# Column groups instead of token tiles: the order of the products that pick up the leader's rows of the last batch

## The chip, the cores and the metric

The kernel runs on one core of a Trainium2 chip. The metric is the device time of one execution in microseconds (us), as the median of several executions. The profile is of one execution of its own. The engines have one instruction stream each: TensorE (PE in the rows; its weight loads are the rows PEld), VectorE (DVE), ScalarE (ACT), GpSimd (POOL) and SyncE (SP, which here issues DMAs only). A letter q behind an engine's name is its sequencer, which issues DMAs.

## The reference

Three stages follow each other, all in float32.

```python
# 1. attention, batch 4, heads 8, sequence 576, head size 64
scores = scale * q @ k.T + min(-(cum[:, None] - cum[None, :]), 0)   # causal; cum = cumsum(max(s, 0))
attn   = softmax(scores);  x = (attn @ v)                           # -> [2304 tokens, 512]
# 2. eight experts, each token goes to one of them
e = argmax(x @ w_gate);  p = softmax(x @ w_gate)[e]
x = p * (max(x @ w1[e], 0) @ w2[e])                                 # w1 512x1024, w2 1024x512
# 3. dense
h = max(x @ w_in, 0);  out = (h * h) @ w_out                        # 512 -> 2048 -> 512
```

## The kernel before

**Three stages in one program.** The attention stage (class `Attention`) works through four batches of 576 tokens. The expert stage (class `Moe`, `run`) takes the experts one after the other, with a fixed room of columns for each (400 for the first, then 360, 336 and so on), in eight steps of 128 hidden units: `l1` (lines L1460 to L1462) makes twelve products `he`, `act1` (L1469, L1470) turns them into the operands `hhe` and `hle`, `l2` (L1479 to L1481) makes twelve products `y_e`. The dense stage has the same form (`hd`, `y_d`). In these stages the order of the instructions on each engine is the order in which the code is written.

**Float32 in two parts.** Every float32 operand of a product is split into a high part, which ScalarE copies, and a low part, which VectorE makes by subtracting the high part from the source. A product then needs high with high, high with low, and low with high. `split` (L1389 for the high part, L1390 for the low) does it for the weights of the next step: `wae_1h`, `wae_1l` are the parts of the first expert's second block of w1, `wbe_1h`, `wbe_1l` of w2.

**The first expert starts early.** The expert with the most tokens in the first three batches, the leader, goes first, so that its tokens of those batches can be fetched before the gate of the last batch is done. That is what `Moe.first` does. The leader's 400 columns of x, transposed, are built in four banks of PSUM, `acc(k)` for k from 0 to 3, one for each 128 of the 512 features; in the rows they are `ttacc` (k = 0, 1) and `pvacc` (k = 2, 3). First a product with zeros opens each bank (L1266). Then the rows fetched from the first three batches are turned into place by products with a diagonal of ones (`s4aux`, tasks `xgt`). Last come the rows of the fourth batch, still in SBUF: the tasks `take` multiply their features by a matrix `Pones` of zeros and ones, 256 columns wide, that VectorE makes from the tokens' places (task `at`, L1323). There are five tiles t of tokens, four of 128 (features `xhb`, `xlb`) and one of 64 (`hhb`, `hlb`), hence ten products for each k, all on line L1262. Then ScalarE makes the high part `xhf` of each bank (tasks `xh`, L1341) and VectorE the low part `xlf` (tasks `xl`, L1344): these are the x that the first products `he` read.

The features' own parts are made before: ScalarE makes `xhb`, `hhb` by column group c (tasks `bh`, L1310), VectorE the low parts `xlb`, `hlb` (tasks `bl`, L1313, two for each c). VectorE makes the last batch's places with the chain of the gate: `g_lg`, `g_oh`, products `ork` on TensorE, `base`, `g_slot`, `slots`. It also makes the order of the other seven experts (tasks `order`, L1056 to L1090, and `order2`, L1097 to L1104), which SyncE reads before it fetches the next expert's token list (`idt`).

**What sets the order there.** The tasks of the attention stage and of `Moe.first` are put in order by a planner (`Steps.run`), at build time. Each task has an engine, an estimated duration, the tasks that it needs, the buffers that it uses and a due time; a task inherits an earlier due time from those that need it. The planner keeps a clock of its own, takes the engine with the earliest free task, and of those that can start within 60 ns of each other the one due first. Where TensorE would wait for more than 250 ns of the planner's time, it puts in products that nobody reads (the filler, L330: `ofill`, 256 columns, from `mrow` and `identb`, written off at 110 ns each), as many as fill 80% of the gap.

**Waits in the program.** An engine works its stream in order. A task's needs set the planner's order only; the waits in the program follow from what an instruction reads and writes.

Of the kernel before, what the change touches and what calls it, by code (L numbers as in the profile page):

```python
# [30 lines left out]
class Steps:  # L31
# [37 lines left out]
    def run(self):  # L69
# [37 lines left out]
        while ready:  # L107
# [8 lines left out]
            for e, l in best.items():  # L116
# [4 lines left out]
                            key=lambda x: x[1]["due"])  # L121
                first.append((t, op["due"], e, op))
            t, _, e, op = min(first, key=lambda x: x[:2])
            gap = t - free[e] if e == "PE" and self.fill and not any(self.keep) else 0
            if gap > self.GAP:
# [878 lines left out]
class Moe:  # L1004
# [192 lines left out]
    def first(self, at):  # L1197
# [4 lines left out]
        b, C, N = at.B - 1, CAPS[0], self.NTOK  # L1202

        LO = C - 256
        assert LO * E <= b * at.S
        V = nc.vector
        due = at.PACE * (at.NH + self.LATE)
# [48 lines left out]
        ua = lambda k: ("pv" if k // 2 else "tt", ("acc", k))  # L1256
        left = [2 * (len(self.chunks(C)) + 5)] * 4

        def put_in(k, cols, w, ones):

            left[k] -= 1
            nc.tensor.matmul(out=at.tile(*ua(k))[:, cols], lhsT=w[:, 128 * k:128 * k + 128], rhs=ones,  # L1262
                             start=False, stop=not left[k])

        for k in range(4):
# [6 lines left out]
               need=["leadr"] + put(b - 1), use=[("idt", 0)])  # L1272
# [3 lines left out]
        for c, m in self.chunks(C):  # L1276
            st.add(("xg", c), {"Pool": 1040}, lambda c=c, m=m: self.gather("f", got["idt"], c, m, b * at.S, xg()[:, c]),
                   need=["idt"] + [("gx", i, j) for i in range(b) for j in range(2)], use=[("idt", 0), ug], lat=3000)
            w = "ab"[c // 2]
            h, l = (lambda w=w, x=x, c=c: at.tile(w + x, ("x", c), [128, 512], F32R) for x in "hl")  # L1280
            u = [(w + x, ("x", c)) for x in "hl"]
            at.act(("xgh", c), 540, lambda c=c, m=m, h=h: nc.scalar.copy(out=h()[0:m], in_=xg()[0:m, c]),
                   need=[("xg", c)], use=[ug, u[0]])
            at.dve(("xgl", c), 560, lambda c=c, m=m, h=h, l=l: V.tensor_tensor(
                out=l()[0:m], in0=xg()[0:m, c], in1=h()[0:m].bitcast(F32), op=ALU.subtract), need=[("xgh", c)],
                use=[ug] + u, due=due)
# [15 lines left out]
        for c in range(4):  # L1302
# [13 lines left out]
            ub = [("xb", b), ("xh", "b"), ("hh", "b")]  # L1316
# [3 lines left out]
        ones = lambda t: at.tile("P", ("ones", t), [128, 512], F32R)[:, LO:C]  # L1320
        up = lambda t: ("P", ("ones", t))
        for t in range(5):
            at.dve(("at", t), 140, lambda t=t: V.tensor_scalar(  # L1323
                out=ones(t), in0=places(), scalar1=at.slot[:, t:t + 1], scalar2=None, op0=ALU.is_equal),
                need=["places", ("g", "slot", b)], use=[up(t), ug])

        def take(t, k):
            for x in "hl":
                w = at.tile("x" + x, "b")[:, t, :] if t < 4 else at.tile("h" + x, "b")[0:64]
                put_in(k, slice(LO, C), w, ones(t)[0:w.shape[0]])  # L1330

        ub = [(x + y, "b") for x in "xh" for y in "hl"]
        bl = [("bl", c, i) for c in range(4) for i in range(2)]
        for t in range(3):
            at.pe(("take", t), 8 * 256, lambda t=t: [take(t, k) for k in range(4)], need=[("at", t)] + bl + [("zero", k) for k in range(4)],
                  use=ub + [up(t)] + [ua(k) for k in range(4)])
        x = lambda: got.setdefault("x", None) or got.update(x=self.xtiles("f")) or got["x"]
        for k in range(4):
            at.pe(("take", 3, k), 4 * 256, lambda k=k: [take(t, k) for t in (3, 4)],
                  need=[("at", t) for t in (3, 4)] + bl + [("take", 0)], use=ub + [up(3), up(4), ua(k)])  # L1340
            at.act(("xh", k), C, lambda k=k: nc.scalar.copy(out=x()[0][:, k, 0:C], in_=acc(k)),  # L1341
                   need=[("take", 3, k)] + [("take", t) for t in range(3)] + [("xgt", c, k) for c, _ in self.chunks(C)],
                   use=[ua(k), ("xh", 0)])
            at.dve(("xl", k), C, lambda k=k: V.tensor_tensor(out=x()[1][:, k, 0:C], in0=acc(k),  # L1344
                                                             in1=x()[0][:, k, 0:C].bitcast(F32), op=ALU.subtract),
                   need=[("xh", k)], use=[ua(k), ("xh", 0), ("xl", 0)], due=due)

        for g in range(2):
            for i in range(2):
                at.dma(("w", g, i), lambda eng, g=g, i=i: self.wload(0, g, got["e"], parts=(i,), eng=eng), 1460, queues=("ACT",),  # L1350
                       need=["leada"] + after, use=[("s4", (g, i))], due=due + 20000 * g)
        self.ws = {}
        for i, w in enumerate("ab"):
            use = [("s4", (0, i))]
            t = lambda h, w=w: at.tile(w + h, "w", [128, 512], F32R)
# [3 lines left out]
            def low(i=i, t=t, vw=vw, src=src):  # L1359
# [4 lines left out]
                   need=[("w", 0, i)], use=use + [(w + "h", "w")])  # L1364
# [34 lines left out]
    def dense_load(self, i):  # L1399

        nc = self.nc
        NP = self.F2 // 128
        first, f = i < NP, i % NP
        src, dst = (self.w_in, self.win) if first else (self.w_out, self.wout)
        if first:
            dst = dst[:, :, 128 * f:128 * f + 128]
            view = src[:, 128 * f:128 * f + 128].rearrange("(k p) f -> p k f", p=128)
        else:
            dst = dst[:, f, :].unsqueeze(1)
            view = src[128 * f:128 * f + 128, :].unsqueeze(1)  # L1410
        if src.dtype not in (mybir.dt.int64, mybir.dt.uint64):
            nc.sync.dma_start(out=dst, in_=view)
            return
        n = dst.shape[1]

        if i < 2 * NP - 4:
            at = 2 * (i % (NP // 2)) if first else NP - 4 + 2 * (i % 2)
            st = self.wout[:, at:at + 2, :].rearrange("p a d -> p (a d)").bitcast(I32)
        else:
            st = self.s4.tile([128, 1024], I32, tag="s4", name=f"f64_{i}")  # L1420
        st = st.rearrange("p (n m t) -> p n m t", n=n, t=2)
        nc.sync.dma_start(out=st.rearrange("p n m t -> p n (m t)"), in_=view.bitcast(I32))
        self.f64[i] = (st, dst)
# [50 lines left out]
    def l2(self, key, hh, hl, C, acc, first, last):  # L1474
        nc = self.nc
        _, (wh, wl) = self.wq.pop(key)
        for m in range(4):
            c = slice(128 * m, 128 * m + 128)
            nc.tensor.matmul(out=acc[m][:, 0:C], lhsT=wh[:, c], rhs=hh[:, 0:C], start=first, stop=False)  # L1479
            nc.tensor.matmul(out=acc[m][:, 0:C], lhsT=wh[:, c], rhs=hl[:, 0:C], start=False, stop=False)  # L1480
            nc.tensor.matmul(out=acc[m][:, 0:C], lhsT=wl[:, c], rhs=hh[:, 0:C], start=False, stop=last)  # L1481
# [264 lines left out]
```

## Time and profile before

| | us |
|---|---|
| median of 3 executions | 914.91 |
| lowest, highest | 914.04, 917.18 |
| the profiled execution, whole time | 913.02 |
| its span, first to last instruction | 911.4 |
| TensorE busy | 841.1 (92%) |
| VectorE busy | 662.0 (73%) |
| ScalarE busy | 494.8 (54%) |
| GpSimd busy | 325.8 (36%) |
| granted TensorE clock, mean | 0.970 of full speed |

The profiled execution lies 1.9 us below the median and its span 1.6 us below its own time, so differences are read from the trace and applied to the median. A line such as `245.60 0.41 PE L1262 MATMUL ttacc<-Pones,xhb 128*128 128x256 f32 x1` is one instruction, or a run of equal ones: start, duration from the first start to the last end, engine, line of the program, operation, what is written and read, shape, count; in square brackets the idle time of the engine just before it and what ended that. Since products are pipelined, the distance between two starts tells what one costs, not the duration printed. The place of the change lies between 239 and 255 us of the span.

### The profile page before, as it was taken

The numbers are of one execution on the slowest core, as the hardware profiler recorded it, in microseconds if no ns is written. First come the engines' busy times: TensorE is split into PE (matmuls) and PEld (weight loads), VectorE is DVE, ScalarE is ACT, GpSimd is POOL, SyncE is SP. The second block draws the span as 40 slices with busy tenths as digits, with TensorE's granted clock in tenths as the row PEclk, the third lists the DMA queues.
The fourth block names the chain that finished last, engine by engine and source line by source line (L and its number), as shares of the span: only waits on it lengthen the run. The fifth ranks groups of instructions, "written<-read, shape, count | busy, mean of one in ns | idle before, by whom it ended". The sixth has DMA issues, their size and how long they took to land. (4 is left out here: it accounts for less than half of the span.)

```text
span 911.4 us, 17086 instructions
## 1 busy us (share of the span) xinstructions
PE 841.1 (92%) x6451; PEld 714.9 (78%) x6451; DVE 662.0 (73%) x1214; ACT 494.8 (54%) x1001; POOL 325.8 (36%) x354
## 2 busy tenths in 40 slices
PE   4888868877999999999999999999999999999994
PEld 3566656656799999999999778888888888888894
DVE  8989988996859789888988884544464456444673
ACT  4779758886444444554555444544454444444562
POOL 9876667575355436554522540100010002000100
PEclk9999988988899999999999999999999999999998
DMA  6787978940576586677562300000000001000100
GB/s 146 146 153 172 165 142 174 190 98 18 167 235 192 160 265 195 211 234 265 188 200 73 116 1 1 15 33 1 1 34 13 1 1 47 1 1 1 47 1 26
DMA packets 155489, 94.03 MB, mean 103 GB/s; under 512 B 115292, under 2 KB 140342, under 8 KB 155402
## 3 DMA queue, kind: packets, MB, share of 16 engines
q1 hardware_dynamic: 143410, 78.00, 32.8%
q0 software_dynamic: 4096, 10.19, 3.4%
q10 hardware_dynamic: 7896, 4.69, 1.8%
q8 instruction: 52, 0.85, 0.4%
q14 instruction: 35, 0.29, 0.1%
HBM read 70.16 MB, written 10.02 MB: 88 GB/s over the span
## 5 line engine op out<-in xcount | busy, mean ns | idle before, releaser
L1599 POOL DMA_INDIRECT out_dram<-o,ids x18 | 18.5, 1025 | 342.0 <-ACT o L1596 299.1
L1542 DVE TENSOR_TENSOR sqd<-hd,rld 128x512 f32<-128x512 f32 (+1 forms) x80 | 50.9, 636 | 112.9 <-ACT rld L1540 112.1
L1540 ACT ACTIVATE rld<-hd 128x512 f32<-128x512 f32 (+1 forms) x80 | 44.4, 555 | 129.6 <-PE hd L1462 126.8
L1546 DVE TENSOR_TENSOR ald<-sqd,ahd 128x512 fp32r<-128x512 f32 (+1 forms) x80 | 51.1, 639 | 51.5 <-ACT ahd L1545 50.8
L1545 ACT CAST ahd<-sqd 128x512 fp32r<-128x512 f32 (+1 forms) x80 | 46.3, 579 | 75.4 <-DVE sqd L1542 75.4
L722 POOL TENSOR_TENSOR L<-P,H 128x512 f16<-128x512 f32 x59 | 72.4, 1239 | 27.2 <-ACT H L721 22.0
L1442 POOL TENSOR_TENSOR lf<-lf,pw 128x512 f32<-128x512 f32 x32 | 50.1, 1567 | 73.9 <-DVE pw L1441 55.3
L719 ACT ACTIVATE P<-tt 128x512 f32<-128x512 f32 x96 | 54.5, 595 | 19.7 <-PE tt L667 17.5
L755 PE MATMUL pv<-v,H 128*128 128x65 f16 (+1 forms) x896 | 59.0, 199 | 4.4 <-ACT xb L785 1.8
L1469 ACT ACTIVATE hhe<-he 128x400 fp32r<-128x400 f32 (+7 forms) x64 | 27.9, 436 | 61.7 <-PE he L1462 61.5
L755 PEld LDWEIGHTS <-H 128*128 128x128 f16 x896 | 50.0, 100 | 11.2 <-issue 8.0
L755 PE MATMUL pv<-v,L 128*128 128x65 f16 x448 | 55.2, 197 | 3.4 <-issue 1.4
L667 PE MATMUL tt<-qB,kB 128*128 128x128 f16 (+3 forms) x352 | 57.5, 238 | 0.0
L721 ACT CAST H<-P 128x512 f16<-128x512 f32 x96 | 56.6, 619 | 1.2 <-DVE v L449 0.8
L666 PE MATMUL tt<-qA,kA 128*128 128x128 f16 (+3 forms) x352 | 53.7, 239 | 1.6 <-ACT P L719 1.4
L755 PEld LDWEIGHTS <-L 128*128 128x128 f16 x448 | 43.9, 103 | 4.1 <-issue 1.5
L601 DVE TENSOR_REDUCE tops<-mxb 128x1 f32<-128x128 f32 (+1 forms) x96 | 43.5, 499 | 4.8 <-remote 2.6
L1167 POOL DMA_INDIRECT xg<-x_dram,idt x20 | 20.8, 1040 | 69.5 <-PE xps L1177 63.7
L577 PE MATMUL mxb<-kB,qB 128*128 128x128 f16 (+3 forms) x128 | 33.6, 325 | 12.2 <-ACT qB L499 4.8
L1470 DVE SCALAR_TENSOR_TENSOR hle<-he,hhe 128x400 fp32r<-128x400 f32 (+7 forms) x64 | 30.8, 480 | 13.8 <-ACT hhe L1469 12.9
L667 PEld LDWEIGHTS <-kB 128*128 128x128 f16 x368 | 34.0, 105 | 8.4 <-issue 4.1
L666 PEld LDWEIGHTS <-kA 128*128 128x128 f16 x368 | 35.0, 105 | 6.4 <-issue 2.5
(699 smaller groups left out, 3072.6 us busy)
## 6 DMA issues: line engine op xcount, KB each, us to landing
w0s<-in_moe_w_dram SPq DMA_DIRECT2D x30, 512.0 KB
w1s<-in_moe_w_dram SPq DMA_DIRECT2D x30, 512.0 KB
wout<-in_moe_w_in_dram SPq DMA_DIRECT2D x16, 512.0 KB
wout<-in_moe_w_out_dram SPq DMA_DIRECT2D x12, 512.0 KB
ldq<-in_q_dram SPq DMA_DIRECT2D x31, 128.0 KB
ldv<-in_v_dram SPq DMA_DIRECT2D x28, 128.0 KB
ldk<-in_k_dram SPq DMA_DIRECT2D x27, 128.0 KB
x_dram<-xb SPq DMA_DIRECT2D x3, 1024.0 KB
```

The lines of the kernel that those rows point to most:

```text
L601: nc.vector.tensor_reduce(out=st[:, at:at + k], in_=ps[:, c:c + w].rearrange("p (k w) -> p k w", k=k), axis=AX.X, op=ALU.max)
L666: nc.tensor.matmul(out=ps, lhsT=kA[:, j], rhs=qA[:, i], start=not on, stop=False)
L667: nc.tensor.matmul(out=ps, lhsT=kB[:, j], rhs=qB[:, i], start=False, stop=not (mask or more))
L719: self.act(("P",) + key, w, lambda: nc.scalar.activation(out=P(), in_=ps(), func=AF.Exp, scale=0.125), need=[T], use=[use, ("P", key), ("H ...
L721: self.st.add(("H",) + key, {"ACT": 0.833 * w + 80}, lambda: nc.scalar.copy(out=H(), in_=P()), need=[("P",) + key], use=[("P", key), ("H", ...
L722: f = lambda e="Pool": (nc.gpsimd if e == "Pool" else nc.vector).tensor_tensor(out=L(), in0=P(), in1=H(), op=ALU.subtract)
L755: nc.tensor.matmul(out=ps[0:M, I, 0:N], lhsT=a, rhs=m, start=(i == 0), stop=(i == len(ops) - 1))
L1442: nc.gpsimd.tensor_tensor(out=lf, in0=lf, in1=pw.bitcast(F32), op=ALU.mult)
L1540: nc.scalar.activation(out=rl[:, 0:n], in_=ps, func=AF.Relu)
L1542: nc.vector.tensor_tensor(out=a[:, 0:n], in0=ps, in1=rl[:, 0:n], op=ALU.mult)
L1545: nc.scalar.copy(out=ah[:, 0:n], in_=a[:, 0:n])
L1546: nc.vector.tensor_tensor(out=al[:, 0:n], in0=a[:, 0:n], in1=ah[:, 0:n].bitcast(F32), op=ALU.subtract)
```

## The change

The products that pick up the last batch's rows are grouped by column group k instead of by token tile t. Before, three tasks did t = 0, 1, 2 for all four k, eight products each, and four tasks did t = 3 and 4 for one k each; all of them needed the low parts of all four column groups. Now there are four tasks of ten products, one for each k, with t from 0 to 4 inside; each needs all five matrices of ones, but the low parts of its own column group only. The due times of the four low parts `xl` are set apart by 4,000 ns and earlier than before. Number, shape and operands of the products are the same.

```diff
-        def take(t, k):
-            for x in "hl":
-                w = at.tile("x" + x, "b")[:, t, :] if t < 4 else at.tile("h" + x, "b")[0:64]
-                put_in(k, slice(LO, C), w, ones(t)[0:w.shape[0]])
+        def take(k):
+            for t in range(5):
+                for x in "hl":
+                    w = at.tile("x" + x, "b")[:, t, :] if t < 4 else at.tile("h" + x, "b")[0:64]
+                    put_in(k, slice(LO, C), w, ones(t)[0:w.shape[0]])
 
         ub = [(x + y, "b") for x in "xh" for y in "hl"]
-        bl = [("bl", c, i) for c in range(4) for i in range(2)]
-        for t in range(3):
-            at.pe(("take", t), 8 * 256, lambda t=t: [take(t, k) for k in range(4)], need=[("at", t)] + bl + [("zero", k) for k in range(4)],
-                  use=ub + [up(t)] + [ua(k) for k in range(4)])
         x = lambda: got.setdefault("x", None) or got.update(x=self.xtiles("f")) or got["x"]
         for k in range(4):
-            at.pe(("take", 3, k), 4 * 256, lambda k=k: [take(t, k) for t in (3, 4)],
-                  need=[("at", t) for t in (3, 4)] + bl + [("take", 0)], use=ub + [up(3), up(4), ua(k)])
+            at.pe(("take", k), 10 * 256, lambda k=k: take(k), need=[("at", t) for t in range(5)] + [
+                ("bl", k, i) for i in range(2)] + [("zero", k)], use=ub + [up(t) for t in range(5)] + [ua(k)])
             at.act(("xh", k), C, lambda k=k: nc.scalar.copy(out=x()[0][:, k, 0:C], in_=acc(k)),
-                   need=[("take", 3, k)] + [("take", t) for t in range(3)] + [("xgt", c, k) for c, _ in self.chunks(C)],
+                   need=[("take", k)] + [("xgt", c, k) for c, _ in self.chunks(C)],
                    use=[ua(k), ("xh", 0)])
             at.dve(("xl", k), C, lambda k=k: V.tensor_tensor(out=x()[1][:, k, 0:C], in0=acc(k),
                                                              in1=x()[0][:, k, 0:C].bitcast(F32), op=ALU.subtract),
-                   need=[("xh", k)], use=[ua(k), ("xh", 0), ("xl", 0)], due=due)
+                   need=[("xh", k)], use=[ua(k), ("xh", 0), ("xl", 0)], due=due - 4000 * (4 - k))
```

The planner answers to this on three engines; SyncE and GpSimd keep their order, and behind the first products `he` every engine has the order of before.

On TensorE, behind the products `ork` of the gate, stand fillers and then the products of the takes. Before there are 22 fillers, and the first takes go through the four banks:

```order
L330 LDWEIGHTS identb_120
L330 MATMUL ofill_1657_5304<-mrow_129,identb_120 128x256
L1262 MATMUL ttacc_0_5096<-Pones_0_5296,xhb_5031 128x256
L1262 MATMUL ttacc_0_5096<-Pones_0_5296,xlb_5118 128x256
L1262 MATMUL ttacc_1_5099<-Pones_0_5296,xhb_5031 128x256
L1262 MATMUL ttacc_1_5099<-Pones_0_5296,xlb_5118 128x256
L1262 MATMUL pvacc_2_5102<-Pones_0_5296,xhb_5031 128x256
```

Now there are 12 fillers, and the takes go through the five tiles for the first bank:

```order
L1262 MATMUL ttacc_0_5087<-Pones_1_5289,xhb_5022 128x256
L1262 MATMUL ttacc_0_5087<-Pones_1_5289,xlb_5109 128x256
L1262 MATMUL ttacc_0_5087<-Pones_2_5291,xhb_5022 128x256
L1262 MATMUL ttacc_0_5087<-Pones_2_5291,xlb_5109 128x256
L1262 MATMUL ttacc_0_5087<-Pones_3_5293,xhb_5022 128x256
L1262 MATMUL ttacc_0_5087<-Pones_3_5293,xlb_5109 128x256
L1262 MATMUL ttacc_0_5087<-Pones_4_5297,hhb_5023 128x256
L1262 MATMUL ttacc_0_5087<-Pones_4_5297,hlb_5110 128x256
L1262 MATMUL ttacc_1_5090<-Pones_0_5285,xhb_5022 128x256
```

Ten fillers went, and the 64-row products, which stood in the last 16 of the 40, now end each group of ten.

On VectorE, from the end of the gate's chain to the first product's low weights, stand before (the low parts of the features, the matrices of ones, the low weights of the first step, `order` and `order2`, the low parts of x):

```order
L1313 TENSOR_TENSOR xlb<-xb_4237,xhb 128x4x128 x2
L1313 TENSOR_TENSOR hlb<-xb_4237,hhb 64x128 x4
L1323 TENSOR_SCALAR Pones_5296<-xbg,g_slot_5160 128x256
L1360 TENSOR_TENSOR alw<-w0s_0_5208,ahw 128x512
L1360 TENSOR_TENSOR blw<-w1s_0_5218,bhw 128x512
L1056 TENSOR_TENSOR key_5368<-base,base_63 128x8
L1097 CAST nf<-o_n 128x8
L1104 CAST o_off<-off 128x8
L1344 TENSOR_TENSOR xlf<-ttacc_5096,xhf 128x400
L1344 TENSOR_TENSOR xlf<-pvacc_5125,xhf 128x400
L1390 TENSOR_TENSOR wae_1l<-w0s_0_5208,wae_1h 128x512
```

and now:

```order
L1323 TENSOR_SCALAR Pones_5285<-xbg,g_slot_5151 128x256
L1313 TENSOR_TENSOR hlb<-xb_4237,hhb 64x128
L1357 TENSOR_TENSOR alw<-w0s_0_5208,ahw 128x512
L1341 TENSOR_TENSOR xlf<-ttacc_5087,xhf 128x400
L1341 TENSOR_TENSOR xlf<-ttacc_5090,xhf 128x400
L1357 TENSOR_TENSOR blw<-w1s_0_5218,bhw 128x512
L1341 TENSOR_TENSOR xlf<-pvacc_5093,xhf 128x400
L1056 TENSOR_TENSOR key_5382<-base,base_63 128x8
L1341 TENSOR_TENSOR xlf<-pvacc_5116,xhf 128x400
L1097 CAST nf<-o_n 128x8
L1104 CAST o_off<-off 128x8
L1387 TENSOR_TENSOR wae_1l<-w0s_0_5208,wae_1h 128x512
```

The matrices of ones moved ahead of the low parts of the second to the fourth column group (the first group's `hlb` even ahead of the products `ork`); three low parts of x moved ahead of `order`, the fourth ahead of `order2`, so that `order2` now stands directly before `wae_1l`. Lines behind the edited place are three lower now.

On ScalarE one thing moved: the load of the leader's number into a register (L1233, from `lead`), before between the copies `xT` and the first `xhb`, now ahead of the last copy `bhx`, and still ahead of the first loads of w1 and w2:

```order
L1282 CAST bhx_5137<-xbg 128x512
L1233 TENSOR_LOAD lead
L1233 ISA x2
L1282 CAST bhx_5204<-xbg 16x512
L1377 ISA
L1377 DMA w0s_0_5208<-in_moe_w_dram 128x4x256
```

## Rows read from the trace of the kernel before

**Rows 1.** Busy time by stretch, behind the place: us; PE, PEld, DVE, ACT, POOL; clock; DMA.

```profile
252.00:300.00 48.00, 48.00 (x275) 47.86 (x275) 35.95 (x56) 22.98 (x43) 24.29 (x16) 1.00 0.71 220
400.00:500.00 100.00, 97.04 (x723) 93.45 (x723) 87.00 (x138) 54.15 (x108) 40.98 (x31) 1.00 0.57 182
```

**Rows 2.** Timeline of TensorE at the place.

```profile
241.08 4.81 PE L330 MATMUL ofill<-mrow,identb 128*128 128x256 bf16 x22 [0.49 <-DVE base L932]
245.60 0.41 PE L1262 MATMUL ttacc<-Pones,xhb 128*128 128x256 f32 x1
245.85 0.28 PE L1262 MATMUL ttacc<-Pones,xlb 128*128 128x256 f32 x1
245.97 0.28 PE L1262 MATMUL ttacc<-Pones,xhb 128*128 128x256 f32 x1
...
249.36 0.38 PE L1262 MATMUL ttacc<-Pones,xhb 128*128 128x256 f32 x1
...
250.22 0.39 PE L1262 MATMUL pvacc<-Pones,xhb 128*128 128x256 f32 x1
...
251.73 0.27 PE L1262 MATMUL pvacc<-Pones,hlb 64*128 64x256 f32 x1
251.93 0.45 PE L1460 MATMUL he<-xhf,ahw 128*128 128x400 f32 x1
...
254.60 0.34 PE L1462 MATMUL he<-xhf,wae_1l 128*128 128x400 f32 x1
```

**Rows 3.** Busy time and granted clock by stretch, at the place.

```profile
238.00:239.00 1.00, 1.00 (x10) 0.93 (x9) 0.88 (x7) 0.24 (x1) 0.00 (x0) 0.94 0.55 201
240.00:241.00 1.00, 0.58 (x20) 0.50 (x19) 0.50 (x4) 0.99 (x2) 0.00 (x0) 0.50 0.63 217
245.00:246.00 1.00, 1.00 (x8) 0.81 (x7) 1.00 (x3) 0.00 (x0) 1.00 (x1) 0.65 1.10 400
250.00:251.00 1.00, 1.00 (x6) 0.68 (x5) 0.72 (x2) 0.49 (x1) 0.00 (x0) 1.00 0.02 1
```

**Rows 4.** Timeline of VectorE at the place.

```profile
240.62 0.20 DVE L931 TENSOR_TENSOR g_s<-ork,base 128x40 f32<-128x40 f32 x1 [0.47 <-PE ork L928]
...
241.47 1.28 DVE L1313 TENSOR_TENSOR xlb<-xb,xhb 128x512 fp32r<-128x512 f32 x2
242.67 0.88 DVE L1313 TENSOR_TENSOR hlb<-xb,hhb 64x128 fp32r<-64x128 f32 x4
243.48 1.53 DVE L1323 TENSOR_SCALAR Pones<-xbg,g_slot 128x256 fp32r<-128x256 f32 x5
244.94 0.68 DVE L1360 TENSOR_TENSOR alw<-w0s,ahw 128x512 fp32r<-128x512 f32 x1
...
246.15 0.15 DVE L1056 TENSOR_TENSOR key<-base,base 128x8 f32<-128x8 f32 x1
...
247.42 0.17 DVE L1097 CAST nf<-o_n 128x8 f32<-128x8 int32 x1
...
248.50 0.17 DVE L1104 CAST o_off<-off 128x8 int32<-128x8 f32 x1
249.99 0.57 DVE L1344 TENSOR_TENSOR xlf<-ttacc,xhf 128x400 fp32r<-128x400 f32 x1 [1.32 <-issue]
...
253.08 0.69 DVE L1390 TENSOR_TENSOR wae_1l<-w0s,wae_1h 128x512 fp32r<-128x512 f32 x1
```

**Rows 5.** Timeline of ScalarE (and its DMA issues, ACTq) at the place.

```profile
234.26 0.40 ACTq L1380 DMA_DIRECT2D w0s<-in_moe_w_dram  x1
...
235.39 1.13 ACT L1282 CAST bhx<-xbg 128x512 fp32r<-128x512 f32 x2
...
249.47 0.49 ACT L1341 CAST xhf<-ttacc 128x400 fp32r<-128x400 f32 x1 [8.32 <-PE ttacc L1262]
...
261.43 0.61 ACT L1389 CAST wae_4h<-w0s 128x512 fp32r<-128x512 f32 x1
```

**Rows 6.** Timeline of SyncE's DMA issues at the place.

```profile
250.74 0.38 SPq L1160 DMA_DIRECT2D idt<-tab  x1
```

## The prediction, made before the changed kernel ran

> **What bounds the kernel now.** I read the stretches first. Behind 252 us TensorE is busy for 48.00 of 48 us and later for 97 of 100, at full clock, in an order that the change leaves alone [rows 1]. So the change is worth what it moves the first product of that stage, the first `he` at 251.93 [rows 2], less what TensorE then waits for in its first few steps. Next I read TensorE's timeline just ahead of it. 22 fillers run from 241.08 to 245.60 at (245.60 − 241.08)/22 = 0.205 us each; the 40 takes follow from 245.60 to 251.93, 6.33 us, and ScalarE, idle for 8.32 us, starts the first high part of x at 249.47 [rows 2, 5]. Third, what the takes waited for: VectorE has the last low part done at 242.67 + 0.88 = 243.55 and the first matrix of ones by about 243.8 [rows 4]. Nothing held the takes between 243.8 and 245.60 but the fillers ahead of them on TensorE's own stream. The reader is to see there that a wait was covered by more work than the wait was long. Why: the granted clock is 0.50 there, the lower level of 1.2 GHz. It is 0.94 on the mean of 238 to 239, 0.50 from then on, and 0.65 on the mean of 245 to 246, so it fell at about 238.9 and rose at 245.7 (0.3 of that us at full clock) [rows 3]. Ahead of the rise TensorE issued 256-column products without a gap for 4.6 us. The planner wrote the fillers off at 110 ns, and they took 205.
>
> **The change, part by part.** All sums are in the profiled execution, 913.02 us with a span of 911.4; they are carried over to the median of 914.91 as differences.
>
> *Start of the takes.* The products `ork` and the chain on VectorE ahead of the fillers are the same; the one thing put in, the first group's `hlb` (0.2 us each, 0.88 for four), fits into the 0.47 us for which VectorE waits for `ork` [rows 4]. If it did not fit, the fillers would start up to 0.2 us later. So 12 fillers run from 241.08 to 241.08 + 12 × 0.205 = 243.55. Is the data there? Places are done when VectorE goes on at 241.47; five matrices of ones take 1.46 us (243.48 to 244.94), so the last stands at 243.0 and each is ready before TensorE asks for it. Takes start at 243.55 instead of 245.60, 2.05 us earlier; the fillers still hold them.
>
> *The takes themselves.* At full clock they cost 6.20 us: 6.08 from 245.85 to 251.93 and 0.12 for the first, as the pair from 245.85 to 245.97 shows; the 0.25 us of the first itself is still at the lower clock [rows 2]. A change between 128-row and 64-row products costs extra: one round of two and two takes 0.86 us (249.36 to 250.22) against 4 × 0.12 = 0.48. There are four such rounds in both orders, so the 6.20 us stay, 1.55 for each k. Now the first 2.15 us, up to the rise at 245.7, pass at half clock and do 1.07 us of that work. 5.13 us remain: the takes end, and `he` may start, at 250.83, 1.10 us earlier than 251.93.
>
> *The clock's rise* is the unknown in this. I take 245.7 as before, because TensorE issues 256-column products without a gap from 241.08 on in both kernels; only what they multiply changes at 243.55. The bounds are a rise at the start of the takes, which saves another 1.07 us, and none until the takes are through, which is the slow rival below. In the Trainium skill, "TensorE: Matmul & The Clock Gate", Part 1, the clock is throttled by default and released by busy time, not by a number of matmuls, and the moment varies from run to run. By that rule ten fillers fewer do not put off the rise, and the sum stays at 250.83, while other executions would spread around it; the trace, with one rise in this place, agrees with the first part and cannot show the second.
>
> *High and low parts of x.* Each bank is now complete by itself, 1.55 us apart instead of 0.86. By the sums the takes for k = 3 start at 249.28 and their last product ends at 250.9; ScalarE's copy (0.49 us, idle before) is done at 251.43. VectorE has by then the low parts for k = 0 to 2 behind it, the third at 249.4 + 0.04 + 0.49 + 0.04 + 0.57 = 250.5. Then stands `order`, seven small operations, 246.15 to 247.42, of which some 1.15 us hold up what comes next [rows 4]; the fourth low part runs from 251.6 to 252.15. The first `he` needs it only for its eleventh product, at 250.83 + 10 × 0.19 = 252.7 (0.19 us apiece, from (254.60 − 251.93)/14 in [rows 2]). So this is hidden, with 0.5 us to spare.
>
> *What is late next: `wae_1l`.* Behind the fourth low part stands `order2`, from 247.42 to 248.50 + 0.08, 1.16 us [rows 4]. Before it ran in VectorE's idle time ahead of 249.99. Now it ends at 253.25, and `wae_1l` follows at 253.25 to 253.94, later than before (253.08) although the takes end earlier. TensorE asks for it in its fifteenth product, 2.67 us behind the first `he` (251.93 to 254.60): at 253.50. It waits 0.45 us, until 253.95, against 254.60 before. Gain: **0.65 us**. Behind that VectorE has free time (35.95 of 48 us busy) and the steps go on as before [rows 1].
>
> *ScalarE's register load* moves behind the copies `bhx`. In the old place nothing shows of it, and here ScalarE's sequencer runs ahead: it issued the load of `w0s` at 234.26 while the copies before it in the stream still ran from 235.39 to 236.5, 2.2 us later [rows 5]. I take nothing. The bounds are nothing and some 0.5 us on the chain to the places, which would shift the fillers' start by as much; a gain is not in it, as VectorE has work all the time there.
>
> *SyncE.* The token list of the next expert was fetched at 250.74 [rows 6]; its register load reads `order`, which is now done at about 251.6 instead of 247.4. So that fetch and the load of `w0s` queued behind it come 1 to 2 us later. That block is first used at 261.43 [rows 5]: hidden by some 7 us. GpSimd loses nothing: its next work waits for the takes' buffers, which come free earlier.
>
> Sum: 913.02 − 0.65 = 912.4 in the profiled execution, 914.91 − 0.65 = **914.3** as median. That is 0.07%. A measurement of this kernel tells about 0.3% (2.7 us) from no change, and the three executions alone are 3.1 us apart.
>
> **The rivals.**
> *The whole 1.1 us arrives*: `order2` delays nothing, because VectorE catches up while TensorE works through `he`. For it: the small operations can overlap; against: seven of them in a row depend on each other, with 0.2 us between starts. Time 914.91 − 1.10 = 913.8.
> *The wait only changes its name*: `wae_1l` comes at or behind 254.6 because `order` and `order2` both stand between the low parts of x and it, and the chain of copies slips by 0.65 us. For it: VectorE has no idle time left between 250 and 254 by my sum; against: it has to slip further than any row shows. Time 914.9.
> *The clock stays down* (the slower side): the 64-row rounds, now spread through the takes, count for less than fillers, and the rise comes only when the takes are through. Then 2 × 6.20 = 12.4 us put the first `he` at 243.55 + 12.4 = 255.95, 4.0 us later: 918.9. It decides from a rise at 247.9: there (247.9 − 243.55)/2 of the work is lost to the lower clock and `he` starts at 251.93 as before. For it: ten products of certain effect at the place of the rise are gone. Against: from 249.36 to 251.73 the same rounds ran, and the clock stayed at 1.00 [rows 3].
> By the same rule of the Trainium skill ("TensorE: Matmul & The Clock Gate", Part 1) this rival does not come, since 64-row products keep the engine busy too; no row shows a rise during such products.
>
> **How the numbers follow.** Forecast (gain of 0.3 to 0.9 us) 0.45; the whole gain or a little more 0.20; the wait changes its name (gain of −0.3 to 0.3) 0.25; the clock stays down for all or part of the takes 0.10. All but the far end of the last lie within 0.3%. Faster by over 0.3% would need 2.7 us, which no term reaches: only the scatter of executions can give it, 0.05. Slower by over 0.3% has the far end of the last case and the scatter, 0.05. Within 0.3%: 0.90. For the range I take the terms' own (−1.1 to +0.3 us, some way towards +4.0) and the scatter of the three executions (0.9 below and 2.3 above the median, less for a median): 912.7 to 916.7.
>
> **What would show it.** In the changed profile 12 fillers from about 241.1; the first take at 243.5 to 243.7; four groups of ten, the first slow, the granted clock back at 1.00 near 245.7; high parts of x 1.55 us apart; the first `he` near 250.8; a short wait of TensorE for `wae_1l` near 253.5 and this product at 254.0; busy time by stretch behind 260 as before. The forecast is wrong if the first `he` lies behind 251.9, if TensorE waits for a low part of x, or if the difference between the times is more than that at `he`, which would mean that a later stage answers to the shift.

## The result and the profile after

The changed kernel takes 924.70 us as median of 4 runs (923.36 to 927.28), the kernel before, in the same comparison, 914.89 us (914.04 to 917.18). The ratio is 1.0101 with a 95% interval of 1.0071 to 1.0132: slower by 1%, 9.8 us between the medians. (A ratio here is not the quotient of the two medians, which is 1.0107.) Of all executions reported here one of the seventh experiment's eight (928.96 us) ran in a slower state: the ratio there leaves it out, the median of 922.46 us does not. The prediction of no measurable change, 914.3 us in a range up to 916.7, was wrong. The profiled execution of the changed kernel took 927.28 us, its span is 925.8 us, 14.4 us more than before.

Where the 14.4 us lie is read from two places on TensorE's timeline: the start of the fillers ahead of the takes, and the first product `he` (L1457 now).

```profile
245.12 2.74 PE L330 MATMUL ofill<-mrow,identb 128*128 128x256 bf16 x12 [0.58 <-DVE base L932]
...
247.51 0.56 PE L1262 MATMUL ttacc<-Pones,xhb 128*128 128x256 f32 x1
...
254.95 0.27 PE L1262 MATMUL pvacc<-Pones,hlb 64*128 64x256 f32 x1
255.15 0.45 PE L1457 MATMUL he<-xhf,ahw 128*128 128x400 f32 x1
...
265.27 0.70 PE L1458 MATMUL he<-xlf,ahw 128*128 128x400 f32 x1 [8.02 <-DVE xlf L1341]
...
267.02 0.70 PE L1459 MATMUL he<-xhf,wae_1l 128*128 128x400 f32 x1
```

- Up to the fillers: 245.12 against 241.08 [rows 2], +4.0 us. This is scatter of the attention stage from one execution to the next. The second experiment below, which changes nothing ahead of this place, starts its fillers at 244.65; the third, which has the changed kernel's code up to there, at 242.70, the fourth at 241.05.
- From the fillers to `he`: 255.15 − 245.12 = 10.03 us, before 251.93 − 241.08 = 10.85 [rows 2], −0.8 us. There are 12 fillers, as forecast.
- From `he` to the end: 925.8 − 255.15 = 670.65, before 911.4 − 251.93 = 659.47, **+11.2 us**. In it lies a wait of 8.02 us for a low part of x, `xlf`, that did not exist before.

So the whole loss stands behind `he`, within the first steps. The stretches show the same (busy time in us by engine, PE, PEld, DVE, ACT, POOL; granted clock; DMA):

```profile
252.00:300.00 48.00, 39.93 (x210) 38.34 (x210) 35.73 (x52) 17.70 (x34) 20.93 (x16) 0.89 0.47 149
400.00:500.00 100.00, 96.61 (x728) 94.35 (x727) 88.29 (x142) 52.27 (x105) 43.40 (x33) 1.00 0.67 215
```

TensorE is busy for 39.93 of 48 us where it was 48.00, at a mean clock of 0.89 instead of 1.00; from 400 to 500 us it works as before [rows 1]. What `xlf` waited for stands on VectorE's timeline:

```profile
254.70 0.16 DVE L1056 TENSOR_TENSOR key<-base,base 128x8 f32<-128x8 f32 x1
...
255.29 0.17 DVE L1086 MAX8 top<-key 128x8 f32<-128x8 f32 x1
255.49 8.97 DVE L1087 CAST ki<-top 128x8 int32<-128x8 f32 x1
264.50 0.17 DVE L1088 TENSOR_SCALAR o_e<-ki 128x8 int32<-128x8 int32 x1
...
264.65 0.57 DVE L1341 TENSOR_TENSOR xlf<-pvacc,xhf 128x400 fp32r<-128x400 f32 x1
...
266.28 0.69 DVE L1387 TENSOR_TENSOR wae_1l<-w0s,wae_1h 128x512 fp32r<-128x512 f32 x1
```

A cast of eight columns, the fifth operation of `order`, took 8.97 us. The reader is to see that no idle time is printed for it: by the profile VectorE was busy, so the table of busy times alone hides the wait (35.73 us busy in the stretch against 35.95 before). What runs beside it on GpSimd tells more. First the kernel after, then the kernel before, where the cast stood earlier:

```profile
255.34 9.09 POOL L1607 MEMSET y<- 128x2664 f32 x4 [1.38 <-PE pvacc L1262]
```

```profile
246.94 0.17 DVE L1087 CAST ki<-top 128x8 int32<-128x8 f32 x1
...
252.11 9.14 POOL L1610 MEMSET y<- 128x2664 f32 x4 [2.51 <-ACT xhf L1341]
```

GpSimd zeroes the accumulator `y` in four instructions, from the moment that the takes are through. In the kernel after the cast starts 0.15 us behind the start of this zeroing and ends at 264.46, the zeroing at 264.43. In the kernel before `order` and `order2` were done at 248.67 [rows 4], 3.4 us before the zeroing began.

The stop also costs clock (granted clock in the column before the last two):

```profile
262.00:264.00 2.00, 0.00 (x0) 0.00 (x0) 2.00 (x1) 0.00 (x0) 2.00 (x2) 0.50 0.00 0
...
268.00:270.00 2.00, 2.00 (x8) 1.98 (x7) 1.25 (x3) 0.00 (x0) 1.52 (x2) 0.50 0.96 296
270.00:272.00 2.00, 2.00 (x10) 1.99 (x9) 0.71 (x2) 1.01 (x2) 0.78 (x1) 0.71 0.85 250
```

TensorE, idle from 257.25 on, comes out of the stop at 0.50, the lower level of 1.2 GHz, and is back at 2.4 GHz 0.84 us before 272 (a mean of 0.71 is 42% of 2 us at full clock), at 271.2. From 265.27 to 271.2 half the work is lost, 2.95 us. 8.02 + 2.95 = 11.0 of the 11.2 us.

### The profile page after: what moved, and what is told of

It reads as the page before. It is cut to its first block, busy times and chain, and to the rows that moved or that the text cites. A ratio compares the mean times of both kernels' runs of the same rounds, so it can differ in the third digit from the quotient of the medians.

```text
span 925.8 us, 17065 instructions
## 1 busy us (share of the span) xinstructions
PE 842.5 (91%) x6441; PEld 715.4 (77%) x6441; DVE 671.0 (72%) x1214; ACT 495.4 (54%) x1001; POOL 326.5 (35%) x354
```

## The experiments

Theory: VectorE's one-source operations on SBUF (CAST, TENSOR_SCALAR) cannot run while GpSimd's zeroing does, as if both used one access to SBUF; two-source operations can. The change moved `order` into the zeroing. Rivals: VectorE is late there for another reason; the grouping of the takes itself costs. The kernel before had a median of 913.49 us beside the first four runs, 904.86 beside the fifth and sixth and 913.29 beside the seventh (three different chips of this kind), so each ratio is against the runs of the kernel before of its own comparison, and the absolute times expected for the fifth and sixth were some 9 us too high from the start. "`he` to the end" is the span less the start of the first `he`, from the trace.

| run | zeroing, us | longest instruction of `order`, us | longest wait of TensorE behind `he`, us | `he` to the end against before, us | ratio of times, 95% interval |
|---|---|---|---|---|---|
| after | 9.09 | 8.97 | 8.02 | +11.2 | 1.0101 (1.0071 to 1.0132) |
| e1, two sources | 9.13 | 0.17 | 0.25 | +0.6 | 0.9987 (0.9958 to 1.0016) |
| e2, before with `order` late | 9.10 | 7.39 | 8.68 | +8.9 | 1.0108 (1.0055 to 1.0160) |
| e3, half the zeroing | 4.66 | 4.53 | 3.59 | +7.4 | 1.0057 (1.0025 to 1.0089) |
| e4, `order` first | 9.13 | 0.17 | none | +0.1 | 1.0022 (0.9995 to 1.0050) |
| e5, zeroing in pieces | 10.05 | 9.92 | 8.98 | +11.5 | 1.0103 (1.0065 to 1.0140) |
| e6, groups alone | 9.13 | 0.18 | none | 0.0 | 1.0009 (0.9988 to 1.0029) |
| e7, casts alone rewritten | 9.10 | 8.78 | 7.32 | +8.8 | 1.0074 (1.0031 to 1.0118) |

**e1: the same place, other operations.** The kernel after, in which six one-source operations of `order` and `order2`, three casts and three with scalars, get a second source, a constant tile:

```diff
-        nc.vector.tensor_copy(out=ki, in_=top)
+        nc.vector.tensor_tensor(out=ki, in0=top, in1=self.zf, op=ALU.add)
-        nc.vector.tensor_scalar(out=self.ord[0], in0=ki, scalar1=E - 1, scalar2=E - 1,
-                                op0=ALU.bitwise_and, op1=ALU.bitwise_xor)
+        nc.vector.scalar_tensor_tensor(out=self.ord[0], in0=ki, scalar=E - 1, in1=self.seven,
+                                       op0=ALU.bitwise_and, op1=ALU.bitwise_xor)
...
```

> The changed kernel with the same order of instructions; the six operations of order and order2 that had one source in SBUF (two casts, three operations with scalars, one cast of the offsets) take a second source, a small constant. Port theory: a one-source operation of VectorE cannot start while GpSimd zeroes y (9.09 us from 255.34 on in the changed profile), a two-source one can. So the 8.97 us cast is gone, the operation takes about 0.2 us, TensorE waits for the fourth low part not at all and for wae_1l 0.2 to 0.8 us, and the time is 914.3 (913 to 916). Rival, the cast waited for its data or for a transfer: an operation of the same place still takes about 9 us, 923 to 926. Rival, the grouping by columns costs by itself: no stop, but 920 or more.

Measured: 912.94 us against 913.49. In the trace (VectorE, then GpSimd and TensorE) the order of the instructions is that of the kernel after, and nothing stops:

```profile
255.76 0.17 DVE L1092 TENSOR_TENSOR ki<-top,cst 128x8 int32<-128x8 f32 x1
...
256.12 0.57 DVE L1346 TENSOR_TENSOR xlf<-pvacc,xhf 128x400 fp32r<-128x400 f32 x1
...
257.00 0.16 DVE L1105 TENSOR_REDUCE over<-over 128x1 f32<-128x8 f32 x1
...
257.76 0.68 DVE L1392 TENSOR_TENSOR wae_1l<-w0s,wae_1h 128x512 fp32r<-128x512 f32 x1
```

```profile
255.61 9.13 POOL L1612 MEMSET y<- 128x2664 f32 x4 [1.40 <-PE pvacc L1267]
```

```profile
255.41 0.45 PE L1462 MATMUL he<-xhf,ahw 128*128 128x400 f32 x1
...
258.50 0.45 PE L1464 MATMUL he<-xhf,wae_1l 128*128 128x400 f32 x1 [0.25 <-DVE wae_1l L1392]
```

The write of `ki` now takes 0.17 us 0.15 us behind the start of the same zeroing, where the cast took 8.97. The loss is gone with the form of six small operations, nothing else moved. Besides it shows the wait for `wae_1l` that the prediction had at 0.45 us; it is 0.25. (A TENSOR_REDUCE has one source too, and runs beside the zeroing in 0.16 us: not every one-source form is held.)

**e2: the kernel before, with `order` late.** One need more, the takes as before, all 22 fillers:

```diff
-        at.dve("order", 1500, self.order, need=["lead", ("g", "s1", b), ("at", 4)], due=due + self.OD)
+        at.dve("order", 1500, self.order, need=["lead", ("g", "s1", b), ("at", 4), ("xl", 3)], due=due + self.OD)
```

> The kernel before, takes and all, with one need added: order waits for the fourth low part of x. Port theory: order now falls into the zeroing of y, which starts when the takes end (252.11 to 261.25 in the profile of before); its cast stops until about 261.2, wae_1l comes at about 263, TensorE waits some 8 us and then runs for a while at the lower clock: 923 to 927. Rival, the grouping by columns costs by itself: this kernel has no grouping, so 915 to 917 (fifteen small operations late, 2.4 us at most).

Measured: 924.91 us against 913.49, a loss of the same size without the change's grouping. VectorE's, GpSimd's and TensorE's rows:

```profile
256.60 0.17 DVE L1086 MAX8 top<-key 128x8 f32<-128x8 f32 x1
256.81 7.39 DVE L1087 CAST ki<-top 128x8 int32<-128x8 f32 x1
...
265.66 0.68 DVE L1390 TENSOR_TENSOR wae_1l<-w0s,wae_1h 128x512 fp32r<-128x512 f32 x1
```

```profile
255.07 9.10 POOL L1610 MEMSET y<- 128x2664 f32 x4 [2.04 <-ACT xhf L1341]
```

```profile
244.65 3.78 PE L330 MATMUL ofill<-mrow,identb 128*128 128x256 bf16 x22 [0.49 <-DVE base L932]
...
254.89 0.45 PE L1460 MATMUL he<-xhf,ahw 128*128 128x400 f32 x1
...
266.40 0.70 PE L1462 MATMUL he<-xhf,wae_1l 128*128 128x400 f32 x1 [8.68 <-DVE wae_1l L1390]
```

The cast begins 1.74 us into the zeroing and lasts until its end (264.20 against 264.17): its length is what is left of the zeroing, not a size of its own. The MAX8 just ahead of it, which has one source in SBUF as well, ran inside the zeroing in its usual 0.17 us.

**e3: half the zeroing.** The kernel after, in which the second half of the columns of `y` is not zeroed:

```diff
-            nc.gpsimd.memset(self.y[:, m, :], 0.0)
+            nc.gpsimd.memset(self.y[:, m, 0:(N + CAPS[1]) // 2], 0.0)      # 1332 of 2664 columns
```

> The changed kernel with only the first half of the columns of y zeroed (the second half is not). Port theory: the zeroing takes 4.5 us instead of 9.1, the cast stops for 4.4 us, TensorE waits about 3.5 us for the fourth low part, and the clock has less or no time to fall: 917 to 920.5. Rival, the cast waited for something else: 923 to 926.

Measured: 918.66 us against 913.49, +0.57%. The cast again lasts exactly to the end of the zeroing (257.40 against 257.38):

```profile
252.87 4.53 DVE L1087 CAST ki<-top 128x8 int32<-128x8 f32 x1
```

```profile
252.72 4.66 POOL L1607 MEMSET y<- 128x1332 f32 x4 [0.68 <-PE pvacc L1262]
```

The wait fell from 8.02 to 3.59 us, by 4.43, the zeroing by 4.43. Most of the rest of the +7.4 us in its trace is clock: TensorE came out of the shorter stop, at 258.21, at half clock as well, and 264 to 266 us has a mean of 0.79 (58% of 2 us at full clock, so the rise is at 264.8): (264.8 − 258.2)/2 = 3.3 us.

```profile
258.21 0.70 PE L1458 MATMUL he<-xlf,ahw 128*128 128x400 f32 x1 [3.59 <-DVE xlf L1341]
```

```profile
258.00:260.00 2.00, 1.75 (x5) 1.22 (x5) 1.83 (x10) 0.72 (x2) 0.00 (x0) 0.50 0.11 2
...
264.00:266.00 2.00, 2.00 (x10) 1.99 (x10) 1.20 (x2) 0.70 (x2) 0.00 (x0) 0.79 1.02 348
```

**e4: the groups, with `order` early.** `order` and `order2` get due times 20,000 ns earlier in the kernel after.

> The changed kernel with an earlier due time for order and order2, which the planner now puts between the matrices of ones, ahead of all low parts of x. Port theory: no one-source operation is left in the zeroing of y, no stop, nothing late ahead of wae_1l, so the first he counts in full: 912.5 to 915.5 (the matrices of ones come 2.3 us later, which may take the gain of 1.1 us back). Rival, the grouping by columns costs by itself: 920 or more.

Measured: 915.03 us against 913.49, the same as before within the interval. `order` starts at 241.97, its cast runs at 242.77, and nothing stops. But the planner now puts 35 fillers ahead of the takes (12 in the kernel after):

```profile
241.05 6.62 PE L330 MATMUL ofill<-mrow,identb 128*128 128x256 bf16 x35 [0.51 <-DVE base L932]
...
253.70 0.45 PE L1457 MATMUL he<-xhf,ahw 128*128 128x400 f32 x1
```

From the fillers to `he` that is 12.65 us, 1.8 more than before: what the stop had cost is saved, and the 35 fillers take back more than the 12 had given.

**e5: the zeroing in 32 pieces.** Does VectorE get in between two instructions of GpSimd?

```diff
-            nc.gpsimd.memset(self.y[:, m, :], 0.0)
+            for p in range(8):
+                nc.gpsimd.memset(self.y[:, m, W * p:W * p + W], 0.0)      # W = 333
```

> The kernel after, with the zeroing of y cut from 4 instructions of 2664 columns into 32 of 333 columns (some 0.29 us each, from 9.09/32). Theory A, the port is given up between two GpSimd instructions: the cast of `order` waits for the end of one piece at most, each one-source step of `order` and `order2` up to 0.3 us, together below 2 us, hidden but for some 1 us: 912 to 917 us, TensorE waits for the fourth low part under 2 us. Theory B, the waiting VectorE instruction gets in only when GpSimd has nothing more to issue: the cast runs some 9 us until the end of the zeroing, TensorE waits about 8 us as in the kernel after: 921 to 927 us. For B: in the kernel after the cast began 0.15 us behind the first of four zeroings and ended with the last.

Measured: 915.95 us against 904.86. Theory B there holds. The cast started at 244.45, behind the first piece's start, and waited through all others, until 254.37 (the zeroing, 10.05 us from 244.30, ends at 254.35):

```profile
244.45 9.92 DVE L1087 CAST ki<-top 128x8 int32<-128x8 f32 x1
```

```profile
255.18 0.70 PE L1458 MATMUL he<-xlf,ahw 128*128 128x400 f32 x1 [8.98 <-DVE xlf L1341]
```

The summary of the zeroing's instructions, shortest, median and longest in ns, first and last start:

```profile
L1609 POOL MEMSET y<- x32: 382/385/387, 244.3 to 254.0; 128x333 f32 x32
```

They start (254.0 − 244.3)/31 = 0.313 us apart and last 0.385, so each begins before the one ahead has ended. Whether it is this overlap that keeps VectorE out, or a preference for GpSimd, was not separated. The trace of before speaks for the overlap: at 308 us (see below) VectorE gets in between two GpSimd operations that lie 0.07 us apart. But those are other operations on both engines.

**e6: the groups, with the due times of before.** Only the products and their needs as in the change; the four `xl` keep the due times that they had:

```diff
-                   need=[("xh", k)], use=[ua(k), ("xh", 0), ("xl", 0)], due=due - 4000 * (4 - k))
+                   need=[("xh", k)], use=[ua(k), ("xh", 0), ("xl", 0)], due=due)
```

> The column groups of the kernel after, but the due times of the four low parts of x as before: `order` then stands ahead of the first low part of x, `order2` between the second and the third, and 28 fillers stand ahead of the takes instead of 12. Theory A (the loss comes only from one-source VectorE instructions that fall into the zeroing of y, which starts when the last take ends): `order` runs before the zeroing, and so does `order2`; no stop, the first `he` within 2 us of the kernel before counted from the products of the gate, 913 to 917 us. Rival B (the grouping itself, by the order of its takes or copies, costs): 920 us or more, with a wait of TensorE behind the takes of over 5 us.

Measured: 905.93 us against 904.86, the same. 28 fillers, 5.83 us from 235.19; `he` at 247.07, the zeroing from 247.25, and `order2` done at 246.27 (VectorE, then GpSimd):

```profile
246.10 0.17 DVE L1104 CAST o_off<-off 128x8 int32<-128x8 f32 x1
```

```profile
247.25 9.13 POOL L1607 MEMSET y<- 128x2664 f32 x4 [3.65 <-issue]
```

From the fillers to `he` it is 11.88 us, 1.0 more than before, and from `he` on nothing is lost. The grouping costs nothing that the times can tell and gains nothing; the loss of the change hangs on its other half, the due times of `xl`, by which `order` fell behind the third low part. (These due times alone, without the grouping, were not run; the second experiment puts `order` there by another means.)

**e7: which operations?** As e1, but with the two integer TENSOR_SCALAR of `order` left as they were.

> As e1_two_inputs, but the two TENSOR_SCALAR of `order` (`o_e` and `o_n`, integer, one source in SBUF) are as in the kernel after; the three casts keep their second source. Theory A, any such one-source VectorE instruction waits for GpSimd: the first TENSOR_SCALAR that starts behind the begin of the zeroing takes some 8.8 us instead of 0.17, `xlf` and TensorE wait for it as in the kernel after, 921 to 927 us. Theory B, only a cast (or a change of type) is held up: no instruction of `order` takes over 0.3 us and the time is that of e1, 911 to 916 us.

Measured: 922.46 us against 913.29. Now `ki`, with two sources, passes inside the zeroing, and the instruction behind it stops:

```profile
253.93 0.17 DVE L1092 TENSOR_TENSOR ki<-top,cst 128x8 int32<-128x8 f32 x1
254.13 8.78 DVE L1093 TENSOR_SCALAR o_e<-ki 128x8 int32<-128x8 int32 x1
...
254.28 8.64 DVE L1346 TENSOR_TENSOR xlf<-pvacc,xhf 128x400 fp32r<-128x400 f32 x1
```

```profile
253.78 9.10 POOL L1612 MEMSET y<- 128x2664 f32 x4 [0.33 <-PE pvacc L1267]
```

```profile
263.01 0.70 PE L1463 MATMUL he<-xlf,ahw 128*128 128x400 f32 x1 [7.32 <-DVE xlf L1346]
```

So it is not the change of type in a cast. CAST and TENSOR_SCALAR have one source in SBUF in common, but that alone is not it either: MAX8 in e2 and TENSOR_REDUCE in e1 have one too and were not held. What is shown is which forms wait. The low part `xlf` behind it is drawn as 8.64 us: it is queued in VectorE behind the one that waits, since in e1 the same operation took 0.57 beside the zeroing.

None of these kernels is measurably faster than the kernel before. The best, e1, is at 0.9987 with 1 inside its interval.

## Why the prediction was wrong

**The step that failed** is the cost of `order` in its new place. The prediction said "Then stands `order`, seven small operations, 246.15 to 247.42, of which some 1.15 us hold up what comes next", and let the fourth low part run 251.6 to 252.15. The 0.17 us of each operation were read where GpSimd was not zeroing, and carried to a place where it was: in the forecast's own times the takes end at 250.83, so the zeroing starts about 251.0 and `order` runs from 250.5 to 251.6. The term of 1.15 us measured 9.95, from the first operation at 254.70 to the start of `xlf` at 264.65. The sentence "GpSimd loses nothing: its next work waits for the takes' buffers, which come free earlier" was right about the zeroing, which came with the end of the takes (only the fetch behind it then stood 3.7 us for the late token list), and it was the moment to ask the reverse: what does GpSimd's work do to VectorE's, if both now start with the end of the takes?

**No rival named it.** One of the forecast's own signs of being wrong did point there: "if TensorE waits for a low part of x" came true, with 8.02 us. The second rival had the right place, `order` between the low parts of x and the next step, and put 0.65 us on the slip. The slower side was given to the clock during the takes, which did not happen: full clock was back at 250.7, 0.5 us into the second of the four groups and 5.6 us behind the start of the fillers, 1.0 later than forecast (4.6).

```profile
250.00:251.00 1.00, 1.00 (x6) 0.78 (x5) 0.15 (x1) 0.49 (x1) 0.78 (x3) 0.65 1.05 396
```

**There was a sign in the trace of before.** At 308 us the low part of a weight, 0.69 us in [rows 4], takes 1.79 beside a GpSimd operation, VectorE first:

```profile
308.35 1.79 DVE L1390 TENSOR_TENSOR wae_6l<-w0s,wae_6h 128x512 fp32r<-128x512 f32 x1
```

```profile
308.28 1.31 POOL L1442 TENSOR_TENSOR lf<-lf,pw 128x512 f32<-128x512 f32 x1
```

It is no single case. From 300 to 457 us the trace of before has 82 such low parts of weights: the 26 that began while a GpSimd TENSOR_TENSOR was running took 0.93 to 1.82 us and ended 0.54 to 0.56 us behind its end; the other 56 took 0.69 at most. So the two engines do get in each other's way, there with two-source operations on both sides. There the wait was for one GpSimd operation only: this one ends at 309.59 and VectorE's at 310.14, while GpSimd's next is running already:

```profile
309.66 1.62 POOL L1443 TENSOR_TENSOR win<-win,lf 128x512 f32<-128x512 f32 x1
```

The sign was left out, and so the cost of the moved operations was not bounded from above.

The rule is in the Trainium skill, "SBUF — State Buffer", section "Who interferes with whom": VectorE shares one pair of SBUF ports with GpSimd; `copy`, `cast` and `tensor_scalar` can run in modes that take it, and then whoever issues first holds it while the other "fully blocks"; a `tensor_tensor` with both inputs in SBUF only contends with a GpSimd instruction that reads SBUF, and `tensor_reduce` on this chip never does. The runs agree on which forms are held and which are not: the cast 8.97 us and TENSOR_SCALAR 8.78 beside a zeroing, which only writes; TENSOR_TENSOR 0.17 and 0.68 and TENSOR_REDUCE 0.16 beside it; TENSOR_TENSOR 1.79 beside a GpSimd operation that reads. The ports and the modes themselves show in no run. The page speaks of one instruction that is waited for. At 308 us that is so; in the zeroing it was 4, and 32 in e5, and there the measurement decides. By that rule and the row of the zeroing (9.14 us) the forecast would have had a rival of up to 9 us and the clock behind it.

**What held.**
- Twelve fillers, and the takes do not wait: as forecast.
- `he` 1.10 us earlier from the fillers' start: measured 0.82 in the kernel after, 0.77 to 1.85 over the five traces with 12 fillers. But e2, with 22 fillers and the takes as before, has 254.89 − 244.65 = 10.24 us, 0.61 less than before, because its 22 fillers ran in 3.78 us instead of 4.81: a shift of this size comes from where the clock stands as well. That the grouping gives it is not shown.
- High parts of x 1.55 us apart: 253.68 and 255.26, 1.58.

```profile
253.68 0.49 ACT L1338 CAST xhf<-pvacc 128x400 fp32r<-128x400 f32 x1 [1.07 <-PE pvacc L1262]
255.26 0.49 ACT L1338 CAST xhf<-pvacc 128x400 fp32r<-128x400 f32 x1 [1.08 <-PE pvacc L1262]
```

- A short wait for `wae_1l`, 0.45 us: 0.25 in e1. With the stop taken away the change is worth what was predicted, no measurable difference.
- SyncE's fetch of the token list, forecast 1 to 2 us later [rows 6], was 10.8 us later counted from the fillers (265.54 − 245.12 against 250.74 − 241.08), because it reads what `order` writes. TensorE does not wait for it: its list of waits from 255 to 340 us holds only the one for `xlf` (engine, line, waited for: us in total, times, longest).

```profile
265.54 0.38 SPq L1160 DMA_DIRECT2D idt<-tab  x1
```

```profile
PE he L1458 <- DVE xlf L1341: 8.0, 1, 8.0
```

## What to carry to other kernels

When an edit moves small operations on VectorE, look at what GpSimd does at the new place, not only at whether VectorE has time there: eight columns that are cast or combined with a scalar waited here as long as GpSimd's whole run of writes lasted. A due time is enough to bring it about; what protected the kernel before was only that `order` came 3.4 us before the zeroing. If the place can't be changed, give the operations a second source (e1), and price any stop on TensorE at its length plus the half-clock time behind it (8.02 and 2.95 us here).

## What the runs showed of the hardware

- A VectorE operation of 8 columns (0.17 us) lasted 8.97, 7.39, 4.53, 9.92 and 8.78 us in five kernels, each time to within 0.1 us of the end of GpSimd's zeroing. It was a CAST or a TENSOR_SCALAR; MAX8 and TENSOR_REDUCE, with one source too, and operations with two sources ran beside the zeroing in their usual time.
- It waited not for one instruction of GpSimd but for all that stood in a row, 4 or 32 of them (e5), without getting in between. Between two GpSimd operations 0.07 us apart another VectorE operation did get in (308 us, kernel before).
- The wait is drawn as busy time of the waiting instruction, and of instructions queued behind it (`xlf` 8.64 us in e7), without idle time ahead. It is found by durations far from their usual ones, not by the list of waits.
